# mLSTM cell and leaky-ReLU feed-forward: three gate chunks turned without TensorE, one visit moved ahead of a group's products, a new order of small matmuls, and block sums in single instructions

## The chip, the cores and the metric

The kernel runs on one core of a Trainium2 chip. The metric is device time in microseconds (us) of one execution, lower is better; a time is the median of several executions. Engines are named as in the profile: PE is TensorE's matmul, PEld its weight load, DVE is VectorE, ACT is ScalarE, POOL is GpSimd, and SP is SyncE, which here only issues DMAs. A name with a q (SPq, ACTq) is the queue of an engine, where its DMAs are issued.

## The reference

```python
# q, k, v, o_gate: (4, 8, 768, 40); i_gate, f_gate: (4, 8, 768); fp32
for t in range(S):
    m_new = np.maximum(f_gate[:, :, t] + m, i_gate[:, :, t])
    f_stab = np.exp(f_gate[:, :, t] + m - m_new)
    i_stab = np.exp(i_gate[:, :, t] - m_new)
    m = m_new
    C = f_stab * C + i_stab * outer(v[t], k[t])      # per batch and head, 40 x 40
    n = f_stab * n + i_stab * k[t]
    denom = max(|n . q[t]|, 1)
    y[t] = sigmoid(o_gate[t]) * (C @ q[t]) / denom
# then, with x = y laid out as (3072 tokens, 320):
h = x @ w_in                  # w_in (320, 2048), held in 64-bit floats
out = max(0.01 * h, h) @ w_out  # w_out (2048, 320), held in 64-bit floats
```

## The kernel before

**Stages.** The 768 steps are cut into six chunks c = 0 to 5 of 128 tokens. For each chunk the kernel computes the cell for four batches (a step s = 4c + b is one chunk of one batch, all 8 heads), and one chunk later the feed-forward for the 512 tokens of that chunk (a group g = c - 1). The order of the work of PE, DVE, ACT and POOL is written out by hand: a main loop runs over c, and inside over the positions i of the feed-forward pieces `ffs[i]` of group c - 1. Between pieces it puts visits to the cell work of chunk c. Each engine takes its instructions in this written order. The DMAs of SP are not in that hand-written order once the first chunk is laid out: the framework's scheduler places them.

**Feed-forward.** From group 1 on, both layers are done in a Strassen-Winograd form with seven products. A group has 28 pieces: positions 0 to 13 are the seven first-layer products, each for n = 0 and 1 (`fast_firsts`, matmuls at L986; in groups 2 to 5 the order is p1, p6, p7, p4, p2, p5, p3), and positions 14 to 27 the seven second-layer products (`fast_units`, matmuls at L865). A first-layer product uses the PE array as two tiles of 64 rows by 128 columns: r = 0 and r = 1 are two halves of the output columns, each with its own copy of x and of the weights in its 64 partitions. A second-layer matmul uses the whole array. Every matmul here is fp32 and shows in the trace as two instructions.

x lies in `xT` as five slots of 64 features. The two halves hold the features in different orders (`SLOTS`), so that the pair of blocks K1, K2 and the rest KX of the Strassen form lie in different slots in the two halves. Therefore each sum of blocks takes three instructions (one of 128 partitions for the slot that both halves share, two of 64 for the other). `sums_of_weights` makes 14 DVE instructions once, at the end of chunk 1 (positions 24 on); `sums_of_x(c)` makes 12 POOL instructions (L968) at the last position of each chunk c from 1 on, which p7, p6 and p4 of the next group read (x3, x2, x4; one of the four sums is in place in `xT`). `gather_x` brings x into `xT` by DMA from the scratch `x_dr`, into which the mixes write.

**Cell.** From chunk 2 on a step has two visits. `u_parts(s)` ("parts") does, for the two halves u of 64 tokens, 16 score matmuls (`score`, L661, 40 rows by 64 columns, 64 wide) and 16 matmuls of the carried state (`carried`, L668, 64 rows by 40 columns, 42 wide; only u = 0 in chunk 5) into two PSUM banks `sd`; then DVE multiplies the scores with the decay weights (L680) and adds to the state (L641). `u_mix(s)` ("mix") does 16 matmuls over all rows (L749, tile pT), and DVE, POOL and DMAs bring the result to `x_dr`. A score of half u uses array rows of half 1 - u and array columns of half u; only head 7 goes to the columns of the other half. A carried matmul of half u uses rows and columns of half u. So there are four quadrants of 64 by 64, (row half, column half).

The visits of a chunk are listed by `cell_units` and placed by `pairs`: after position 1 the parts of steps 0 and 1, after 3 their mixes, after 13 the parts of steps 2 and 3, after 17 `u_gates` and the mixes of steps 2 and 3. What a visit needs is made ahead by `ahead(s)`: the exponentials of the decay weights (`prep_exp`, ACT L490), the transposed k and q (`prep_kq`, DVE L545 and L553), the state times its decay (`state_next`, POOL L637) and k times its gate (`prep_vu`, POOL L510).

**Gates.** `gates(c + 1)` (DVE: two scans and a few small operations) and `gates_exp(c + 1)` (four ACT exponentials, then DMAs of the rows to the scratch `a_dr`, from which `w` and `ea` are spread) run with 32 rows, one per batch and head, and the 128 tokens along the free axis. The visits need them with the tokens on the partitions. `gates_T`, called by `u_gates`, transposes them on PE against an identity (tile tg: two kinds at L346, and at L351 the last value of each half, broadcast to all partitions), and two DVE copies bring them to `gT` (L353) and `gL` (L355, a piece of the tile f0). In chunk 0 and for chunk 1 this is done earlier, with three kinds.

**Buffers.** Cell PSUM tiles (sd, tg, pT, tk, tq, hN, xt, xe) share four banks; feed-forward tiles (ph, po) share four others.

Of the kernel before, what the change touches and what calls it, by code (L numbers as in the profile page):

```python
# [19 lines left out]
def kernel(  # L20
# [49 lines left out]
    KC = Dm // DP  # L70
    SLOTS = ([0, 2, 4, 1, 3], [1, 3, 0, 2, 4])
# [214 lines left out]
    x_dr = dr.tile([NS, Dm, P], F32, name="x_dr")  # L286
    gT, gL, dCs = {}, {}, {}
# [31 lines left out]
    def gates_exp(c):  # L319
        sync = nc.sync if c == 1 else queues[0]  # L320
        bu, a, na = bus[c]
        if c == 0:
            nc.scalar.activation(bu[:BH, 1, :], bu[:BH, 0, :], AF.Exp, bias=a[:BH, P - 1 :], scale=1.0)
            return
        for u in range(2):
            at = ts(u, SL)
            last = SL * (u + 1) - 1
            nc.scalar.activation(bu[:, 2, at], a[:, at], AF.Exp, bias=na[:] if u else 0.0, scale=1.0)
            nc.scalar.activation(bu[:, 1, at], bu[:, 0, at], AF.Exp, bias=a[:, last : last + 1], scale=1.0)
        if c > 0:  # L330
            sync.dma_start(a_dr[c, 0].rearrange("u n t -> n u t"), a[:].rearrange("n (u t) -> n u t", u=2))
            if c > 1:
                sync.dma_start(a_dr[c, 1].rearrange("u n t -> n u t"), bu[:, 2, :].rearrange("n (u t) -> n u t", u=2))
            if 1 < c < NB - 2:
                load_fi(c + 2)
# [6 lines left out]
    def gates_T(c, bu):  # L342
        tg = psc.tile([P, 5, BH], F32, name="tg", tag="c")
        kinds = 3 if c == 1 else 2
        for n in range(kinds):
            nc.tensor.transpose(tg[:, n, :], bu[:BH, n, :], ident[:BH, :BH])  # L346
        gT[c] = wk.tile([P, 3, BH], F32, name="gT")
        if c > 0:
            for u in range(2):
                last = SL * (u + 1) - 1  # L350
                nc.tensor.transpose(tg[:, 3 + u, :], bu[:BH, 2, last : last + 1].to_broadcast([BH, P]), ident[:BH, :BH])  # L351
            gL[c] = f0[:, ts(c % 2, 2 * BH)].rearrange("p (u n) -> p u n", u=2)
        nc.vector.tensor_copy(gT[c][:, :kinds], tg[:, :kinds, :])  # L353
        if c > 0:
            nc.vector.tensor_copy(gL[c], tg[:, 3:, :])  # L355

# [286 lines left out]
    def u_parts(s):  # L643
# [14 lines left out]
        def score(h):  # L658
            for u, toks, rows in subs(s):
                to = toks if h < H - 1 else ts(1 - u, SL)  # L660
                nc.tensor.matmul(  # L661
                    bank[1 - u][to, h, :], lhsT=kqT[rows, 0, ts(h, SL)], rhs=kqT[rows, 1, ts(h, SL)], start=True, stop=True,
                )

        def carried(h):
            for u, toks, rows in subs(s):
                if u < ends:
                    nc.tensor.matmul(  # L668
                        dC[u][:, h].rearrange("p k d -> p (k d)"), lhsT=d["ku"][toks, h],
                        rhs=S_v[s % NL][toks, u, h, :, :V1], start=True, stop=True,  # L670
                    )

        behind = iter(range(H))
        for h, n in ((0, 1), (1, 2), (2, 1), (3, 2), (4, 1), (5, 1), (7, 0), (6, 0)):
            score(h)
            for _ in range(n):
                carried(next(behind))
        for u, toks, rows in subs(s):
            for hs, at in ((slice(0, H - 1), toks), (slice(H - 1, H), ts(1 - u, SL))):
                nc.vector.tensor_tensor(mixed(s)[toks, u, hs], w[toks, hs], bank[1 - u][at, hs], op=ALU.mult)  # L680
# [253 lines left out]
    K1, K2, KX = ((0, 3), (0, 2)), ((1, 4), (1, 3)), (2, 4)  # L934
# [4 lines left out]
    alike = [(slice(0, P), 0, 0, 1)] + [(ts(r, DP), 1, K1[r][1], K2[r][1]) for r in range(2)]  # L939

    def sums_of_weights():

        def each(what):
            for rows, k, a, b in alike:
                a11, a12, a21, a22 = (w5[rows, 2 * i : 2 * i + 2, j] for i in range(2) for j in (a, b))
                s2, s3, s4 = (t[rows, :, k] for t in (s2_at, s3_at, s4_at))
                yield {
                    1: lambda: nc.vector.tensor_tensor(a21, a21, a22, op=ALU.add),
                    2: lambda: nc.vector.tensor_tensor(s2, a21, a11, op=ALU.subtract),
                    3: lambda: nc.vector.tensor_tensor(s3, a11, a21, op=ALU.subtract),  # L950
                    4: lambda: nc.vector.tensor_tensor(s4, a12, s2, op=ALU.subtract),
                }[what]()

        for what in (3, 1, 2, 4):
            yield from each(what)
        for r in range(2):
            rows = ts(r, DP)
            yield nc.vector.tensor_tensor(dw[rows], w5[rows, :2, KX[r]], w5[rows, 2:, KX[r]], op=ALU.subtract)

    def sums_of_x(g):  # L960

        xT = st["xT", g]
        for what in range(4):
            for rows, k, a, b in alike:
                b11, b12, b21, b22 = (xT[rows, j, ts(i, HT)] for j in (a, b) for i in range(2))
                x2, x3, x4 = (t[rows, k] for t in (x2_at, x3_at, x4_at))
                to, left, right = ((x3, b22, b12), (b12, b12, b11), (x2, b22, b12), (x4, b21, x2))[what]
                nc.gpsimd.tensor_tensor(to, left, right, op=ALU.subtract)  # L968

    def fast_firsts(g):  # L970
# [21 lines left out]
        def w_at(i, n, at):  # L992
            return [lambda r, k=k: w5[:, 2 * i + n, at[r][k]] for k in range(2)]
# [4 lines left out]
        def x_at(at, h):  # L998
            return [lambda r, k=k: xT[:, at[r][k], ts(h, HT)] for k in range(2)]
# [4 lines left out]
        def rest(i, n, h):  # L1004
            return [(lambda r: w5[:, 2 * i + n, KX[r]] if i < 2 else dw[:, n], lambda r: xT[:, KX[r], ts(h, HT)])]
# [62 lines left out]
    def cell_units(c):  # L1068
# [5 lines left out]
        if c + 1 < NB:  # L1074
            units.insert(2 * B - 2, (u_gates, c + 1))
# [149 lines left out]
    with tc.manual_schedule(engines={E.PE, E.DVE, E.Activation, E.Pool}):  # L1225
# [22 lines left out]
        pairs = (1, 1, 3, 3, 13, 13, 17, 17, 17)  # L1248
# [4 lines left out]
        for c in range(1, NB + 1):  # L1253
# [5 lines left out]
            waiting, after = [], []  # L1259
            for i in range(n_ff):  # L1260
# [14 lines left out]
                for n in masks.get(i, ()) if 1 < c < NB else ():  # L1275
                    if c * B + n < NS:
                        prep_mask(c * B + n)
                ffs[i]()
# [3 lines left out]
                if c == 1 and i >= 24:  # L1282
                    run(sums, 3)
# [7 lines left out]
                if c + 1 < NB:  # L1291
                    if i == (1, 0, 0)[min(c, 3) - 1]:
                        gates(c + 1)
                    if i == (3, 4, 2)[min(c, 3) - 1]:
                        gates_exp(c + 1)
                upto = min(n_c, sum(p <= i for p in (place if c == 1 else pairs)))
                while done < upto:
                    fn, s = cells[done]
                    fn(s)
                    done += 1  # L1300
                    if fn is u_mix:
                        waiting.append(s)
                    if fn is u_plain and s < 2 * B - 1 or fn is u_parts and s == 2 * B - 1:
                        ahead(s + 1)
                    elif fn is u_mix:
                        after.append(s + 2)
                    elif fn is u_plain:
                        prep_mask(s + 2)
                        ahead(s + 2)
# [52 lines left out]
```

## Time and profile before

| | |
|---|---|
| three runs | 482.84, 487.22 and 485.26 us, median 485.26 |
| the profiled execution | 489.31 us, its span 487.5 us |
| mean granted TensorE clock | 0.979 |
| busy share of the span | PE 96%, PEld 86%, DVE 70%, ACT 42%, POOL 37% |
| PE's share of the chain of work that ended last | 88% (L986 32%, L865 32%, L749 3%, L661 2%, L668 1%) |
| start of the first-layer products in the trace | group 1 at 140.2, group 2 at 211.4, group 3 at 281.8, group 4 at 352.5, group 5 at 422.6 us |

All durations below are from the one profiled execution. The idle time of an engine that is not on the chain costs nothing, and PE counts as busy while any of its matmuls is in flight, so a busy PE can still lose time between matmuls; that is read from start times.

### The profile page before, as it was taken

How to read it: one execution, taken by the hardware profiler on the slowest of the kernel's cores; microseconds unless marked ns; L12 is line 12 of the kernel's file. 1: busy time of each engine (PE TensorE's matmuls, PEld its weight loads, DVE VectorE, ACT ScalarE, POOL GpSimd, SP SyncE). 2: the span in 40 equal slices, each digit the busy share in tenths (PEclk: the TensorE clock that was granted, in tenths of full speed). 3: DMA queues.
4: the chain of work that ended last, by engine and by line, in shares of the span. 5: the costliest groups of instructions: out<-in, count | busy, mean ns of one | idle time of the engine just before them, and what ended most of it. 6: DMA issues, size and time to landing. Idle time of an engine off the chain costs nothing.

```text
span 487.5 us, 14191 instructions
## 1 busy us (share of the span) xinstructions
PE 466.8 (96%) x5715; PEld 420.4 (86%) x5715; DVE 339.2 (70%) x597; ACT 203.0 (42%) x488; POOL 181.2 (37%) x241
## 2 busy tenths in 40 slices
PE   8586999979999999999999999999999999999997
PEld 6475898657779899998899988899988899988997
DVE  4667566758989999788788878688757687104631
ACT  3662698844434641246530446420346411153210
POOL 4232524552356422695023784113773003700020
PEclk9897999979999999999999999999999999999999
DMA  9999775988660494576673685674876212200001
GB/s 121 160 180 218 142 211 104 255 151 178 153 159 15 104 199 89 127 165 140 150 151 93 160 172 119 161 144 93 169 146 131 64 50 66 70 1 1 9 8 40
DMA packets 165329, 59.31 MB, mean 122 GB/s; under 512 B 128592, under 2 KB 156048, under 8 KB 165264
## 3 DMA queue, kind: packets, MB, share of 16 engines
q1 hardware_dynamic: 125232, 51.23, 47.5%
q10 hardware_dynamic: 40032, 7.18, 9.1%
q8 instruction: 45, 0.74, 0.7%
q14 instruction: 20, 0.16, 0.1%
HBM read 51.68 MB, written 6.70 MB: 120 GB/s over the span
## 4 chain that ended last, share of the span: by engine, by line
PE 88%; DMA 3%; DVE 3%; SPq 2%; ACT 2%; issue 1%; DVEq 0%; ACTq 0%
PE ph L986 32%; PE po L865 32%; PE ph L808 7%; PE po L830 6%; PE pT L749 3%; PE sd L661 2%; SPq L92 2%; DMA acts<-in_moe_w_in_dram 2%; PE sd L668 1%; PE tk L579 1%; DMA rb<-in_q_dram 1%; DMA qn<-in_q_dram 1%; PE hN L721 1%; DVE w_in L282 1%; PE xe L796 0%
## 5 line engine op out<-in xcount | busy, mean ns | idle before, releaser
L865 PE MATMUL po<-w_out,acts 128*128 128x160 f32 x640 | 89.1, 300 | 0.0
L865 PEld LDWEIGHTS po<-w_out,acts 128*128 128x128 f32 x640 | 87.3, 190 | 0.6 <-ACT acts L1011 0.3
L986 PE MATMUL ph<-xT,w_in 64*128 64x256 f32 x720 | 82.7, 378 | 0.0
L986 PEld LDWEIGHTS ph<-xT,w_in 64*128 64x128 f32 x720 | 69.3, 187 | 8.8 <-issue 1.0
L1015 DVE TENSOR_TENSOR acts<-acts,ph 128x512 f32<-128x512 f32 x60 | 38.4, 683 | 40.4 <-PE ph L986 40.3
L865 PE MATMUL po<-raw,acts 128*128 128x160 f32 x480 | 66.4, 300 | 0.0
L865 PEld LDWEIGHTS po<-raw,acts 128*128 128x128 f32 x480 | 65.4, 190 | 0.3
L637 POOL TENSOR_TENSOR S<-S,f 40x336 f32<-40x336 f32 x36 | 30.9, 859 | 60.0 <-PE hN L721 24.5
L1019 ACT COPY acts<-ph 128x512 f32<-128x512 f32 x60 | 32.1, 586 | 49.0 <-PE ph L986 49.0
L1011 ACT ACTIVATE acts<-acts 128x1024 f32<-128x1024 f32 x30 | 31.7, 1057 | 44.7 <-DVE acts L1015 35.9
L680 DVE TENSOR_TENSOR qn<-w,sd 64x448 f32<-64x448 f32 x80 | 33.5, 418 | 18.0 <-PE sd L661 7.9
L482 POOL TENSOR_TENSOR w<-w,i 128x512 f32<-128x512 f32 x20 | 26.5, 1334 | 51.9 <-DMA w<-a_dr 43.3
L490 ACT ACTIVATE w<-w,gT 128x64 f32<-128x64 f32 x160 | 41.6, 338 | 9.8 <-POOL vu L510 3.6
L808 PE MATMUL ph<-xT,w_in 64*128 64x256 f32 x320 | 38.5, 394 | 1.8 <-DVE w_in L282 1.8
L830 PE MATMUL po<-w_out,acts 128*128 128x320 f32 x128 | 38.9, 457 | 0.0
L808 PEld LDWEIGHTS ph<-xT,w_in 64*128 64x128 f32 x320 | 32.9, 195 | 4.9 <-ACT kqT L596 1.2
L986 PE MATMUL ph<-acts,w 64*128 64x256 f32 x320 | 36.6, 381 | 0.0
L763 POOL TENSOR_TENSOR xb<-xb,den 128x320 f32<-128x320 f32 x16 | 11.6, 728 | 63.6 <-DVE xb L760 63.6
L986 PEld LDWEIGHTS ph<-acts,w 64*128 64x128 f32 x320 | 30.4, 187 | 3.7
L830 PEld LDWEIGHTS po<-w_out,acts 128*128 128x128 f32 x128 | 24.6, 199 | 10.0 <-issue 1.7
L903 POOL TENSOR_TENSOR y<-y,raw 128x160 f32<-128x160 f32 x10 | 9.7, 965 | 56.2 <-DVE acts L905 44.8
L968 POOL TENSOR_TENSOR acts<-xT 64x256 f32<-64x256 f32 (+1 forms) x30 | 24.2, 820 | 11.7 <-ACT xT L797 8.5
(175 smaller groups left out, 757.3 us busy)
## 6 DMA issues: line engine op xcount, KB each, us to landing
rb<-in_k_dram SPq DMA_DIRECT2D x64, 80.0 KB
rb<-in_q_dram SPq DMA_DIRECT2D x64, 80.0 KB
rb<-in_o_gate_dram SPq DMA_DIRECT2D x64, 80.0 KB
ea<-a_dr SPq DMA_DIRECT2D x32, 128.0 KB
raw<-in_moe_w_out_dram SPq DMA_DIRECT2D x6, 640.0 KB
w<-a_dr ACTq DMA_DIRECT2D x24, 128.0 KB
xT<-x_dr SPq DMA_DIRECT2D x32, 96.0 KB
x_dr<-x SPq DMA_DIRECT2D x64, 40.0 KB
```

The lines of the kernel that those rows point to most:

```text
L482: nc.gpsimd.tensor_tensor(w, w, cm2.unsqueeze(1).to_broadcast([P, H, SL]), op=ALU.add)
L490: yield nc.scalar.activation(w[:, h, :], w[:, h, :], AF.Exp, bias=gT[c][:, 0, bh : bh + 1], scale=1.0)
L637: nc.gpsimd.tensor_tensor(new, old, g, op=ALU.mult)
L680: nc.vector.tensor_tensor(mixed(s)[toks, u, hs], w[toks, hs], bank[1 - u][at, hs], op=ALU.mult)
L808: nc.tensor.matmul(ph[r][:, cols], lhsT=w_row(r, slot, j), rhs=xT[DP * r : DP * (r + 1), slot, cols], start=(slot == 0), stop=(slot == KC ...
L830: nc.tensor.matmul(po[n][:], lhsT=acts[:, f, ts(n, P)], rhs=w_out[:, f, :], start=(f == 0), stop=(f == NF - 1),)
L865: nc.tensor.matmul(bank[:], lhsT=left[:, f, :], rhs=right[:, f, :], start=f == 0, stop=f == KH - 1)
L968: nc.gpsimd.tensor_tensor(to, left, right, op=ALU.subtract)
L986: nc.tensor.matmul(bank[r][:, e, :], lhsT=left(r)[rows, e], rhs=right(r)[rows], start=first and e == 0 and m == 0, stop=e == 1 and m == le ...
L1011: nc.scalar.activation(to, z, AF.Prelu, alpha=0.01)
L1015: nc.vector.tensor_tensor(to[:, 2 * r : 2 * r + 2], to[:, 2 * r : 2 * r + 2], bank[r], op=ALU.add)
L1019: nc.scalar.copy(to[:, 2 * r : 2 * r + 2], bank[r])
```

## The change

Four things are changed.

1. **Gates of chunks 3 to 5.** `u_gates` is no longer listed in chunks 2 to 4. In its place `gates_turned(c + 1)`, after position 10, transposes the two kinds with four DVE transposes of 32 x 64 elements, and `gates_exp` sends the last values of each half through DRAM: one DMA writes 64 values to the scratch `g_dr`, a second reads them back to all 128 partitions into the same piece of f0. In chunks 3 and 4 `gates` moves from after position 0 to after position 2 and `gates_exp` from 2 to 3.
2. **First visits.** In chunks 3 to 5 the parts of steps 0 and 1 come before position 0, not after position 1. In chunk 2 they stay.
3. **Order and place of the small matmuls.** The 32 matmuls of a parts visit follow a written list, one for even and one for odd steps, and in the half u = s mod 2 heads 6 and 7 go to the other columns, not head 7 alone. The DVE multiplications at L680 are cut at the same head.
4. **Single Strassen sums.** K1, K2 and KX are the same slots in both halves (0 and 3, 1 and 4, 2), so that the right half now leaves out a different block of features. `sums_of_weights` makes five instructions, one at each position from 24 on, and `sums_of_x` four, each of 128 partitions.

```diff
+    VISITS = (
+        "c01 s01 c00 s00 c11 c10 s11 c21 s10 c20 c31 s21 c30 s20 c41 c40 s31 c51 s30 c50 c61 s41 c60 s40 c71 c70 s51 s60 s50 s71 s61 s70".split(),
+        "s00 c00 s01 c10 c01 s10 c20 c11 s11 s20 c30 c21 s21 c40 c31 s30 c50 c41 s31 s40 c60 c51 s41 c70 c61 s50 s61 c71 s51 s60 s70 s71".split(),
+    )
...
+    g_dr = dr.tile([NB, BH, 2], F32, name="g_dr")
...
             if c > 1:
                 sync.dma_start(a_dr[c, 1].rearrange("u n t -> n u t"), bu[:, 2, :].rearrange("n (u t) -> n u t", u=2))
+                sync.dma_start(g_dr[c], bu[:, 2, :].rearrange("n (u t) -> n u t", u=2)[:, :, SL - 1])
+                to = f0[:, ts(c % 2, 2 * BH)]
+                sync.dma_start(to, g_dr[c].rearrange("n u -> (n u)").partition_broadcast(P))
+                gL[c] = to.rearrange("p (n u) -> p u n", u=2)
...
+    def gates_turned(c):
+
+        bu = bus.pop(c)[0]
+        g = gT[c] = wk.tile([P, 3, BH], F32, name="gT")
+        for j in range(P // BH):
+            nc.vector.transpose(g[ts(j, BH), :2, :], bu[:, :2, ts(j, BH)])
...
+        to = [[toks if h < 7 - (u == s % 2) else ts(1 - u, SL) for h in range(H)] for u, toks, _ in subs(s)]
...
-        behind = iter(range(H))
-        for h, n in ((0, 1), (1, 2), (2, 1), (3, 2), (4, 1), (5, 1), (7, 0), (6, 0)):
-            score(h)
-            for _ in range(n):
-                carried(next(behind))
+        parts = list(subs(s))
+        for what, h, u in VISITS[s % 2]:
+            {"s": score, "c": carried}[what](int(h), *parts[int(u)])
...
-    K1, K2, KX = ((0, 3), (0, 2)), ((1, 4), (1, 3)), (2, 4)
+    K1, K2, KX = slice(0, 4, 3), slice(1, 5, 3), 2
...
+        a11, a12, a21, a22 = (w5[:, 2 * i : 2 * i + 2, at] for i in range(2) for at in (K1, K2))
+        yield nc.vector.tensor_tensor(s3_at, a11, a21, op=ALU.subtract)
+        yield nc.vector.tensor_tensor(a21, a21, a22, op=ALU.add)
+        yield nc.vector.tensor_tensor(s2_at, a21, a11, op=ALU.subtract)
+        yield nc.vector.tensor_tensor(s4_at, a12, s2_at, op=ALU.subtract)
+        yield nc.vector.tensor_tensor(dw, w5[:, :2, KX], w5[:, 2:, KX], op=ALU.subtract)
...
+        b11, b12, b21, b22 = (xT[:, at, ts(i, HT)] for at in (K1, K2) for i in range(2))
+        for to, left, right in ((x3_at, b22, b12), (b12, b12, b11), (x2_at, b22, b12), (x4_at, b21, x2_at)):
+            nc.gpsimd.tensor_tensor(to, left, right, op=ALU.subtract)
...
-        if c + 1 < NB:
-            units.insert(2 * B - 2, (u_gates, c + 1))
         return units
...
-        pairs = (1, 1, 3, 3, 13, 13, 17, 17, 17)
+        first_pairs = (1, 1, 3, 3, 13, 13, 17, 17)
+        pairs = (-1, -1, 3, 3, 13, 13, 17, 17)
...
+                if i == 0:
+                    visits(-1)
                 ffs[i]()
...
                 if c == 1 and i >= 24:
-                    run(sums, 3)
+                    run(sums, 1)
...
-                    if i == (1, 0, 0)[min(c, 3) - 1]:
+                    if i == (1, 0, 2)[min(c, 3) - 1]:
                         gates(c + 1)
-                    if i == (3, 4, 2)[min(c, 3) - 1]:
+                    if i == (3, 4, 3)[min(c, 3) - 1]:
                         gates_exp(c + 1)
...
+                if c > 1 and i == 10:
+                    gates_turned(c + 1)
+                visits(i)
```

`visits(i)` is the old code that ran the visits due at position i, made a function; `first_pairs` is used in chunk 2 and `pairs` in chunks 3 to 5.

## The prediction

> **What bounds the kernel now.** I read the table of stretches first, with borders at the starts of the groups (columns: us, then busy time and instructions of PE, PEld, DVE, ACT, POOL, then clock, DMA share, GB/s).
>
> ```profile
> 105.00:140.00 35.00, 35.00 (x255) 24.55 (x254) 28.29 (x46) 17.49 (x49) 10.51 (x14) 0.95 0.76 154
> 140.00:211.35 71.35, 71.00 (x901) 66.15 (x900) 63.46 (x105) 27.84 (x71) 35.83 (x43) 1.00 0.54 122
> 211.35:281.84 70.49, 70.49 (x901) 65.78 (x900) 56.66 (x101) 27.53 (x70) 31.54 (x38) 1.00 0.64 140
> 281.84:352.52 70.68, 70.68 (x901) 65.97 (x900) 57.16 (x100) 27.43 (x70) 30.57 (x37) 1.00 0.65 141
> 352.52:422.61 70.09, 70.09 (x833) 65.42 (x832) 44.98 (x80) 22.55 (x50) 26.69 (x36) 1.00 0.40 92
> ```
>
> From 105 to 422.6 us PE is idle for 0.35 us in all, at full clock from 140 (what it is idle behind that is the end of the kernel, which the change doesn't touch). So a DVE or POOL instruction saved buys nothing unless PE waits for it, and each us taken out of PE's own stream is a us of the time. The chain of waits (start, us, what) says the same of the middle of chunk 3:
>
> ```profile
> 248.72 8.89 PE po L865 x64
> 257.61 0.24 PE tg L346 x2
> 257.85 0.12 PE tg L351 x2
> 257.97 2.02 PE pT L749 x64
> 259.98 21.93 PE po L865 x160
> ```
>
> Inside PE's stream three things are left to gain: the tg transposes, the joints between kinds of matmul, and the packing of sd. I take these from start times of single matmuls, since their ends are modelled.
>
> **Part 1, gates off PE.** The timeline of PE in chunk 2:
>
> ```profile
> 186.49 0.30 PE L346 MATMUL tg<-ident,bu 32*128 32x32 f32 x2
> 186.64 0.28 PE L351 MATMUL tg<-ident,bu 32*128 32x32 f32 x2
> 186.84 1.15 PE L749 MATMUL pT<-qn,S 128*64 128x64 f32 x32
> 188.34 1.15 PE L749 MATMUL pT<-qn,S 128*64 128x64 f32 x32 [0.35 <-DVE f L355]
> 189.43 0.81 PE L865 MATMUL po<-raw,acts 128*128 128x160 f32 x4
> ```
>
> From the first tg to the first pT pass 0.351, 0.358 and 0.351 us in chunks 2, 3 and 4. The joint po to tg (0.230 us between starts) is as long as po to pT in chunk 5 (0.229), so these 1.06 us go whole. In chunk 2 alone the second mix waits for tg's PSUM bank, which DVE empties late: its 64 pT take 2.43 us from first to last start against 1.86 elsewhere. Without tg there is no such bank: 0.57 us more. Sum 1.63 us. What could be late next is L919 of DVE, which p7 needs: in chunk 2 its first half ends about 197.1 and p7 would come at 198.2 - 0.9 = 197.3; it just fits, and a miss costs 0.2 us.
>
> The cover of what is added: four DVE transposes of 32x64 per chunk. The nearest rows are a 128x64 copy (L353, 222 ns) and a 128x512 transpose (L545, 693 ns, so about 90 for an eighth): 0.4 to 0.9 us, less the two copies gone (0.43). At position 10 DVE idles 0.58 us before its next add (312.42 in chunk 4) and 1.2 to 1.3 before the ones behind; the bank that this add reads is written again 1 us after its end. I take nothing; if that cover failed, 0.3 us a chunk. The gates' own DVE work (282.2 to 286.1, 3.9 us) moves behind the multiplications of the first two parts, which come earlier: these end at about group start + 5.6 us, the gates at + 9.5, and the mixes want DVE at + 10.4. It fits.
>
> The two new DMAs stand on SP's queue behind the two of a_dr and ahead of load_fi and the eight x_dr writes; the read waits there until the write has landed. SP issues each DMA in 0.3 to 0.6 us, so 0.8 to 1.0 us, plus the wait. No row has such a write; the nearest is x_dr: its last write issued at 339.5, the read that needs it went at 344.6. So the wait is 0 (if the scheduler puts other DMAs between) to 4.7 us. Behind it stand the x_dr writes, then rb, ea and the gathers. SP itself stops at 319.3 to 323.2 in chunk 4, and the gather that matters ends at 347.4, for a group that starts at 352.5. I take nothing, and the rest is a rival. The Trainium skill, "DMA: Bandwidth & Descriptors", on the anatomy of a DMA, gives a fixed cost of about 2.0 us, mostly the receipt of the write (its fit is for GpSimd's path); by it the wait would be 2 us, and that rival would weigh less than half.
>
> **Part 2, first visits moved.** A joint costs by the kinds on its sides: po to ph 229 ns between starts, ph to sd 306, sd to ph 148; two ph steps in one mode are 209 apart, and the first pair of ph after another kind is followed after 320 instead of 216 ns. Before: po, p1, sd, p6. After: po, sd, p1, p6. The joint ph to sd (306) becomes a plain step (209), and one of two slow first pairs (104) goes; po to sd is not in the trace, and I take po to pT's 229. Gain 97 + 104 = 0.20 us, in chunks 3, 4 and 5: 0.60 us. Bounds: 0.3 if po to sd costs 306, 0.8 if it costs sd's 148.
>
> The cover: at 281.8 all that the parts read is there. Exponentials ended at 280.2, the last kqT at 279.6, the last vu (POOL L510) at 276.3; in chunk 5 350.3, 350.3 and 347.0 for a start at 352.5. These follow PE's own second-layer products, so they move with it. The move also delays p6, which reads x2 of the single sums. In chunk 5 these are at their limit today (POOL's timeline, third line is x2):
>
> ```profile
> 350.49 3.06 POOL L968 TENSOR_TENSOR acts<-xT 128x256 f32<-128x256 f32 x3 [1.60 <-DMA rb<-in_o_gate_dram]
> 353.63 2.20 POOL L968 TENSOR_TENSOR xT<-xT 128x256 f32<-128x256 f32 x3
> 355.91 2.21 POOL L968 TENSOR_TENSOR acts<-xT 128x256 f32<-128x256 f32 x3
> ```
>
> They end at 358.1, p6 starts at 357.95 and gets its second slot just in time.
>
> **Part 4, single sums.** POOL: 12 of about 0.8 us become 4 of 128x512. Nearest rows: L482, 128x512, 1.27 us here; two of today's, 1.6. So 9.6 us become 5.1 to 6.4. DVE's 14 (130.2 to 140.6) become 5, about 4 x 1.3 (128x1024, L886 to L919) + 0.9 = 6 us. PE waits for neither today: worth 0. But x2 would be ready 2.3 to 3.5 us before p6.
>
> **Part 3, order of sd.** In one quadrant scores start every 58 ns and carried every 37 ns (per instruction). Before, the two score quadrants carry 14 x 58 = 812 ns a visit, the other two 16 x 37 + 2 x 58 = 708; a pair of visits is at least 1624. Measured from first to last start, the pairs take 1760, 1666, 1668, 1631, 1734 and 1761 ns in chunks 2 to 4 and 1630 twice in chunk 5, which has 96 instructions, not 128. So the score quadrants bind, and not the number of instructions; the excess is the order. After, even and odd visits swap loads: score quadrants (12 + 14) x 58 = 1508 a pair, the others 32 x 37 + 6 x 58 = 1532. With 20 to 60 ns of imperfection I take 1570 against a mean of 1703 (0.13 us by 6) and 1550 against 1630 (0.08 by 2): 0.96, call it 1.0 us. Bounds: -0.3 (a list whose head-of-line blocking is worse than today's) and 1.3. The four single visits of chunk 1 gain nothing: 12 or 14 scores and at most 824 in the other quadrants. The Trainium skill, "TensorEngine Tiling (Array Packing)", on instruction overhead, speaks against this part: about 60 cycles each, so that a narrow matmul lasts like one of 60 columns. By that a carried one costs as much as a score, the new bound would be 38 x 58 = 2204 ns a pair, and today's 36 x 58 = 2088. The measured 1630 to 1761 and the 37 ns refute it here.
>
> **Sum.** 1.63 + 0.60 + 1.0 = 3.2 us. The profiled execution took 489.31 (span 487.5), 4.05 above the median of 485.26; by it the after is 486.1. I put the same saving on the median: **482.1 us**, 0.7% less.
>
> **Rivals.** (a) The new order brings nothing, PE's issue having its own rhythm: 2.2 us saved, 483.0. For: pairs with one list scatter by 130 ns; against: the pairs at 1630 sit exactly on the score bound. Chance 0.15.
> (b) Slower: the read of g_dr blocks SP for 4.7 us, and the delay reaches the gather of x in each of chunks 2 to 4. The sums would end 4.7 us later, with 2.3 to 3.5 us of room before p6: up to 2.4 us of stall three times, 7.2 - 3.2 = +4.0, 489.3. It decides once more than 2.3 us of delay reach the gather. For: SP issues almost without pause, and the gather of chunk 4 went at 347.4. Against: its pause of 3.9 us at 319.3. Chance 0.07, of which a part over +1% needs ACT's queue, where the loads of w wait for a_dr, to slip as well.
> (c) The scheduler places SP's DMAs anew. In chunk 1 PE waits 3.0 us for q at 102.2, whose issue took 2.66 us, and the clock drops behind it. Gone, it is 482.1 - 3 = 479.1; as much longer, 485.1. For: part 3 and the five sums alter the instructions around; against: none of the DMAs there is changed. Chances 0.11 and 0.05.
> (d) The sums or gates do not get off PE's path as said (a bank or DVE late in each of three chunks, 0.5 us each): 482.1 + 1.5 = 483.6. For: L919's thin room in chunk 2; against: no such wait in chunks 3 and 4 today. It shares (a)'s chance.
>
> The forecast, 482.1 within about 1.3, has 0.62. The range reaches down to (c) and up to between (c) and (b): 479.4 to 485.6. About 1% (4.9 us, what three runs spread over 4.4 can tell) bounds the verdict: faster, under 480.4, 0.18 ((c) and the good end of the bounds); slower, over 490.1, 0.06 ((b) with ACT); same 0.76.
>
> **What would show it.** No tg on PE in chunks 2 to 4, and po followed at once by 64 pT within 1.9 us, in chunk 2 too. From the last po of one group to that of the next 69.6 to 69.9 us in groups 2, 3 and 4, which start 70.1 to 70.7 apart now. Pairs of sd at 1.53 to 1.6 us from first to last start, right behind the last po. x2 done 2 us or more before p6. SP may stand 2 to 5 us before the read of g_dr, with no PE wait after it. Wrong would be: PE idle at a group's start (p1 or p6 for DMA or POOL), sd pairs at 1.7 us, or a moved wait at 102 us that outweighs the rest.

## The result and the profile after

| | before | after |
|---|---|---|
| median | 485.19 us (6 runs, 482.84 to 488.41) | 510.05 us (6 runs, 505.79 to 513.06) |
| ratio | | 1.0506, 95% interval 1.0464 to 1.0548 |
| the profiled execution's span | 487.5 us | 511.2 us |
| mean granted TensorE clock | 0.979 | 0.950 |

The kernel became 25 us slower; 3 us less had been forecast. The two profiles are of executions that took 4.1 us (before) and 3.0 us (after) more than these medians. The same table of stretches as in the prediction (columns: us, busy time and instructions of PE, PEld, DVE, ACT, POOL, then clock, DMA share, GB/s), with the borders at the starts of the groups of the kernel after, says where:

```profile
149.20:229.20 80.00, 74.00 (x897) 69.13 (x896) 60.26 (x99) 27.67 (x71) 31.84 (x33) 0.94 0.50 111
229.20:299.20 70.00, 70.00 (x900) 65.60 (x899) 56.79 (x104) 26.19 (x65) 27.75 (x29) 1.00 0.64 133
299.20:376.40 77.20, 73.23 (x897) 68.64 (x896) 57.69 (x102) 28.57 (x76) 26.83 (x31) 0.96 0.65 134
376.40:446.40 70.00, 70.00 (x836) 65.52 (x834) 44.92 (x80) 22.55 (x50) 23.00 (x24) 1.00 0.41 96
```

Chunks 3 and 5 have no idle PE and are shorter than before, as forecast. In chunk 2 PE is idle for 6.0 us and in chunk 4 for 3.97. Right after each idle time the granted clock is lower (0.50 from 193 to 196 us in chunk 2; 0.94 and 0.96 over the two stretches), so that the loss is larger than the idle time: in chunk 2 the next 64 po take 11.45 us, where 64 po took 8.89 in the prediction's chain of waits. Measured from the start of the last po of a group to that of the next (the first column is the start of the last po ahead of group 1):

| us | up to group 1 | chunk 2 | chunk 3 | chunk 4 | chunk 5 | the last group |
|---|---|---|---|---|---|---|
| before | 139.8 | 71.32 | 70.49 | 70.68 | 70.09 | 61.91 |
| after | 148.8 | 80.20 | 69.94 | 77.32 | 69.83 | 61.91 |

What PE waited for is in its table of waits (us in total, times, longest):

```profile
PE tk L595 <- DMA rb<-in_q_dram: 8.8, 2, 5.1
PE xt L812 <- DVE x L725: 8.8, 3, 5.8
PE sd L677 <- issue: 6.0, 1, 6.0
PE po L881 <- DVE acts L935: 3.8, 1, 3.8
```

tk waits in chunk 1 for loads of q (3.0 us in the kernel before), sd in chunk 2, po in chunk 4; xt is in chunk 0 and was there before (8.0). The 6.0 us of sd stand at "issue": between two matmuls of one visit PE waits for no semaphore that the profile shows.

```profile
186.67 6.00 issue
192.68 0.29 PE sd L677
```

What ends just before is a transfer of 16 KB on the queue that the page calls "instruction" (q8): it runs from 189.30 to 191.29 us, and PE goes on 1.4 us later. It is the 17th transfer on that queue. In all six kernels with the write of this change (below) PE stops at the same count of its matmuls (the 2240th in the trace, in one of them the 2241st) and goes on 1.4 to 1.5 us after the transfer has ended. In the others it had ended 1.5 us or more before PE came there, and PE stands at most 0.16 us. So I read the 6.0 us as PE waiting for its own instructions, which are late with the other DMAs; no run tests that alone.

The table of waits of SP's queue has a row that is new:

```profile
SPq L96 <- DMA g_dr<-bu: 30.4, 4, 8.8
```

Four times SP stands before the read of g_dr for the write to land, 7.6 us on average. It is four times and not three: `gates_exp(2)`, in chunk 1, issues the pair too, though the copy from PE's transposes overwrites that gL. The chain of waits in chunk 4 (start, us, what) follows the delay to PE:

```profile
316.55 3.61 DMA S<-in_v_dram
320.17 9.69 DMA g_dr<-bu
...
329.92 4.39 DMA f<-g_dr
...
335.71 4.58 DMA rb<-in_o_gate_dram
...
343.57 6.46 DMA ea<-a_dr
...
359.00 1.22 DVE acts L935
360.22 0.14 issue
360.36 1.67 PE po L881 x5
```

The write of 256 bytes lands 9.69 us after its issue, and everything behind it on the queue comes late; in the end DVE is late with the sum that a second-layer product reads. The packets of 4 bytes themselves take 0.007 to 0.009 us each.

Part 1's step on PE went as planned. In the chain of waits of chunk 3, tg is gone between po and pT:

```profile
266.42 8.89 PE po L881 x64
275.31 2.02 PE pT L765 x64
277.32 4.68 PE po L881 x33
```

### The profile page after: what moved, and what is told of

It reads as the page before. It is cut to its first block, busy times and chain, and to the rows that moved or that the text cites. A ratio compares the mean times of both kernels' runs of the same rounds, so it can differ in the third digit from the quotient of the medians.

```text
span 511.2 us, 14138 instructions
## 1 busy us (share of the span) xinstructions
PE 475.0 (93%) x5703; PEld 428.6 (84%) x5703; DVE 333.5 (65%) x594; ACT 202.6 (40%) x488; POOL 159.9 (31%) x201
## 4 chain that ended last, share of the span: by engine, by line
PE 77%; DMA 12%; SPq 3%; DVE 3%; issue 2%; POOL 1%; ACT 1%; DVEq 0%; POOLq 0%; ACTq 0%
PE po L881 28%; PE ph L988 27%; PE po L846 6%; PE ph L824 6%; DMA rb<-in_q_dram 4%; SPq L96 3%; PE pT L765 3%; PE sd L677 3%; DMA g_dr<-bu 2%; DMA acts<-in_moe_w_in_dram 1%; DMA ea<-a_dr 1%; DMA S<-in_v_dram 1%; PE tk L595 1%; DMA rb<-in_o_gate_dram 1%; DMA f<-g_dr 1%
## 5 line engine op out<-in xcount | busy, mean ns | idle before, releaser
L881 PE MATMUL po<-w_out,acts 128*128 128x160 f32 x640 | 91.6, 305 | 0.0
L881 PEld LDWEIGHTS po<-w_out,acts 128*128 128x128 f32 x640 | 89.9, 194 | 0.7 <-ACT acts L1013 0.3
L988 PE MATMUL ph<-xT,w_in 64*128 64x256 f32 x720 | 82.7, 378 | 0.0
L988 PEld LDWEIGHTS ph<-xT,w_in 64*128 64x128 f32 x720 | 69.2, 187 | 8.6 <-issue 0.6
L881 PE MATMUL po<-raw,acts 128*128 128x160 f32 x480 | 69.6, 308 | 3.8 <-DVE acts L935 3.8
L881 PEld LDWEIGHTS po<-raw,acts 128*128 128x128 f32 x480 | 68.3, 197 | 4.3 <-ACT y L918 4.0
L506 ACT ACTIVATE w<-w,gT 128x64 f32<-128x64 f32 x160 | 41.5, 339 | 38.7 <-DMA rb<-in_k_dram 12.6
L498 POOL TENSOR_TENSOR w<-w,i 128x512 f32<-128x512 f32 x20 | 27.6, 1390 | 78.6 <-DMA w<-a_dr 56.6
L694 DVE TENSOR_TENSOR qn<-w,sd 64x384 f32<-64x384 f32 (+1 forms) x80 | 33.5, 418 | 27.2 <-ACT w L506 10.8
L824 PE MATMUL ph<-xT,w_in 64*128 64x256 f32 x320 | 41.2, 414 | 1.6 <-DVE w_in L286 1.6
L824 PEld LDWEIGHTS ph<-xT,w_in 64*128 64x128 f32 x320 | 34.6, 207 | 6.1 <-ACT kqT L612 1.2
L846 PEld LDWEIGHTS po<-w_out,acts 128*128 128x128 f32 x128 | 24.6, 199 | 10.0 <-issue 1.3
L569 DVE TENSOR_TENSOR qn<-kqT,ea 64x512 f32<-64x512 f32 x32 | 27.6, 862 | 0.8
```

The source lines that it names most:

```text
L498: nc.gpsimd.tensor_tensor(w, w, cm2.unsqueeze(1).to_broadcast([P, H, SL]), op=ALU.add)
L506: yield nc.scalar.activation(w[:, h, :], w[:, h, :], AF.Exp, bias=gT[c][:, 0, bh : bh + 1], scale=1.0)
L569: nc.vector.tensor_tensor(mixed(s)[rows, 1 - r], d["kqT"][rows, 1].rearrange("p (h t) -> p h t", t=SL), d["ea"][rows], op=ALU.mult,)
L824: nc.tensor.matmul(ph[r][:, cols], lhsT=w_row(r, slot, j), rhs=xT[DP * r : DP * (r + 1), slot, cols], start=(slot == 0), stop=(slot == KC ...
L846: nc.tensor.matmul(po[n][:], lhsT=acts[:, f, ts(n, P)], rhs=w_out[:, f, :], start=(f == 0), stop=(f == NF - 1),)
L881: nc.tensor.matmul(bank[:], lhsT=left[:, f, :], rhs=right[:, f, :], start=f == 0, stop=f == KH - 1)
```

## The experiments

### Is it the gates at all

**Gates back on PE**: the kernel after, with `gates_T` as before and without the four transposes, so parts 2 to 4 alone.

```diff
-                sync.dma_start(g_dr[c], ...)
-                sync.dma_start(to, g_dr[c]...partition_broadcast(P))
+            units.insert(2 * B - 2, (u_gates, c + 1))
```

> The changed kernel with its gates turned on PE again: no scratch g_dr, u_gates at position 17; the moved first visits, the new order and the single sums stay. Theory 1 (the way of the last gate values through DRAM costs the time: its write completes 9.7 to 10 us after its issue and the read behind it holds SP for 8 to 9 us, four times): all of the 25 us go, 483 to 486 us, before less the 0.6 us of the moved visits. Theory 2 (the moved visits, the order or the sums make PE wait): it stays above 500 us.

Measured: 484.15 us, ratio 0.9983 (0.9952 to 1.0015). **Part 1 alone** on the kernel before, with `gates` and `gates_exp` at their old positions:

> The kernel before with the gates' part of the change alone: four DVE transposes and the two DMAs through g_dr; first visits, order and sums as before. Theory 1: 503 to 511 us, with PE stalls in chunks 1, 2 and 4 as in the changed kernel. Theory 2: 483.6 us, the 1.6 us of tg saved.

Measured: 502.26 us, ratio 1.0366 (1.0338 to 1.0394), chunks 2 to 5 at 79.91, 70.18, 70.26 and 70.68 us; chunk 4 loses nothing here, against the expectation. So the loss is in part 1. The rest of part 1 was cleared by **no g_dr**: the kernel after, with gL of chunks 3 to 5 from the tile `ea`, which holds the same numbers, by a POOL copy of 128x8 per step.

```diff
-                sync.dma_start(g_dr[c], ...)
-                sync.dma_start(to, g_dr[c]...partition_broadcast(P))
+            if s >= 3 * B:
+                gl = st[s]["gl"] = wk.tile([P, H], F32, name="gl", bufs=4)
+                nc.gpsimd.tensor_copy(gl[:], st[s]["ea"][:, :, SL - 1])
```

> The changed kernel with both g_dr DMAs taken out. The last gate values of chunks 3 to 5 are copied by POOL (128x8, one copy a step) from the tile ea, which already holds them on the right partitions; for chunk 2 they come from PE, as in both kernels. The four DVE transposes stay. Theory 1: 482 to 484 us (before less 1.6 for tg and 0.6 for the joints, at most 0.3 for the order). Theory 3 (the transposes on DVE, or the gates being later, cost): above 490 us.

Measured: 482.30 us, ratio 0.9965 (0.9941 to 0.9990): everything but the two DMAs is harmless, and this kernel has the lowest median of all. The table of stretches, from group 1 on, has no idle PE and no lowered clock:

```profile
134.60:205.40 70.80, 70.80 (x898) 65.91 (x896) 58.82 (x98) 27.74 (x71) 32.06 (x35) 1.00 0.53 124
205.40:275.40 70.00, 70.00 (x898) 65.67 (x896) 57.37 (x105) 27.85 (x71) 28.19 (x34) 1.00 0.64 142
275.40:345.30 69.90, 69.90 (x898) 65.56 (x896) 55.83 (x103) 27.53 (x70) 26.57 (x34) 1.00 0.66 141
345.30:415.20 69.90, 69.90 (x834) 65.55 (x833) 45.39 (x81) 22.55 (x50) 22.51 (x26) 1.00 0.40 94
```

**The same round trip as one row**: a DVE transpose of two 32x32 blocks puts the 64 values into one partition, and the write is one piece of 256 bytes; write, wait and read stay where they are.

```diff
-                sync.dma_start(g_dr[c], bu[:, 2, :]...[:, :, SL - 1])
+                nc.vector.transpose(row, bu[:, 2, :]...)
+                sync.dma_start(g_dr[c].rearrange("u n -> (u n)").unsqueeze(0), row[BH - 1 : BH]...)
```

> The changed kernel with the same two DMAs at the same places in SP's queue, but what is written is one row: two DVE transposes of 32x32 put the 64 last values on one partition, and the write is 256 bytes in one piece instead of 64 pieces of 4 bytes. Theory 1a (it is the 64 small writes that complete late): the write completes in about 1.5 to 2 us as those of a_dr and x_dr do, SP is held for 1 to 2 us, 482 to 487 us. Theory 1b (any write and read through DRAM in SP's queue holds it as long): SP still held 8 us, 500 us or more.

Measured: 483.68 us, ratio 0.9987 (0.9960 to 1.0013). The read goes 1.24 to 1.72 us after the write's issue (8.0 to 10.2 in the kernel after). A round trip through DRAM on SP's queue is therefore not the trouble; this write is.

### Is it SP's wait, or the write itself

So far all fits a queue held by its wait. Two kernels take the wait for the data away and leave the write: **read late**, with the read moved to product 10, behind load_fi and the x_dr writes (three reads, since that for chunk 2 falls away), and **write only**, without any read (gL as in "no g_dr").

```diff
-                sync.dma_start(to, g_dr[c]...partition_broadcast(P))
+        queues[0].dma_start(to, g_dr[c]...partition_broadcast(P))
```

> The changed kernel with the read of g_dr moved from its place right behind the write to the turning of the gates (product 10 of the group), so that SP issues load_fi and the x_dr writes in between; none for chunk 2, whose gL comes from PE. The writes of 64 pieces of 4 bytes stay, four of them. The output stays the same. If SP's standing before the read is the harm (theory 1): 482 to 486 us, the writes still completing 8 to 10 us after their issue, and the stretches of chunks 2 and 4 at 70 to 71 us instead of 80 and 77. If the slow write also holds up the DMAs behind it (rival): 495 us or more, with PE still waiting for rb in chunk 1.

> The changed kernel with the four writes of g_dr kept, without the reads; gL of chunks 3 to 5 from the ea tile by a 128x8 copy of POOL per step, as in the run 'ea'. Theory 1 (only the wait of the read costs): the time of 'ea', 482.3 us, within 1%. Rival (the 64 small pieces themselves hold up other DMAs): over 488 us, and rb of chunk 1 lands late as in the changed kernel.

Measured: 500.52 us, ratio 1.0335 (1.0299 to 1.0372) for read late, and 500.62 us, ratio 1.0339 (1.0304 to 1.0374) for write only. Theory 1 fell: without the read most of the loss stays. The table of stretches of write only, in pieces of 2 us, shows what the write does (issued at 169.12 us, the last completion at 179.1; the two last columns are DMA share and GB/s):

```profile
168.10:170.10 2.00, 2.00 (x22) 1.78 (x22) 1.96 (x3) 0.24 (x1) 0.10 (x1) 1.00 0.62 156
...
172.10:174.10 2.00, 2.00 (x22) 2.00 (x20) 1.86 (x7) 1.40 (x3) 0.00 (x0) 1.00 0.20 6
174.10:176.10 2.00, 2.00 (x20) 1.71 (x18) 2.00 (x3) 0.00 (x0) 0.00 (x0) 1.00 0.08 15
176.10:178.10 2.00, 2.00 (x24) 1.51 (x24) 2.00 (x4) 0.00 (x0) 0.00 (x0) 1.00 0.06 7
178.10:180.10 2.00, 1.28 (x88) 1.14 (x88) 2.00 (x3) 0.11 (x1) 0.00 (x0) 1.00 0.01 4
180.10:182.10 2.00, 0.00 (x0) 0.00 (x0) 1.89 (x6) 1.90 (x5) 0.00 (x0) 1.00 0.31 89
```

From 172 to 180 us all 16 DMA engines together move 4 to 15 GB/s, though SP had issued six more loads by 172.4 us and ACT one (w<-a_dr, 170.43). By the semaphore updates in the trace SP's first two land 9.0 and 9.5 us after their issue, its other four and ACT's 12.2 to 13.4. Even the other queue stands. Then SP itself stops, with nobody reading g_dr:

```profile
SPq L96 <- DMA g_dr<-bu: 17.8, 3, 6.3
```

Its next DMA is issued at 179.12 us, when the write has completed; it takes over the write's semaphore, so I read the row as a wait for that semaphore to come free (from the numbers in the trace; no kernel tested it).

**Write apart** is write only, with 512 bytes between the 64 values.

```diff
-    g_dr = dr.tile([NB, BH, 2], F32, name="g_dr")
+    g_dr = dr.tile([NB, BH, 2, P], F32, name="g_dr")
...
+                sync.dma_start(g_dr[c, :, :, 0], ...)
```

> As 'write_only', but each of the 64 values of 4 bytes goes to a place of its own, 512 bytes from the next; before, they stood in 512 bytes together. If the pieces are slow since they fall into the same few lines of memory, all 16 completions come within 2 to 3.5 us of the issue, as those of the a_dr writes; if each piece of 4 bytes is slow by itself, the last still comes at 8 to 10 us. Time 482 to 484 us under either.

Measured: 483.43 us, ratio 0.9971 (0.9941 to 1.0002): 17.2 us less than write only, by nothing but the addresses. (Before, the 64 values stood in 256 bytes, not in 512 as the expectation has it.) The same table of stretches, with the write issued at 164.78 us:

```profile
163.80:165.80 2.00, 2.00 (x22) 1.80 (x20) 1.94 (x4) 0.31 (x1) 0.05 (x1) 1.00 0.58 151
...
167.80:169.80 2.00, 2.00 (x22) 1.82 (x20) 1.89 (x6) 1.25 (x3) 0.00 (x0) 1.00 0.87 212
169.80:171.80 2.00, 2.00 (x20) 1.81 (x18) 2.00 (x3) 1.60 (x5) 0.00 (x0) 1.00 0.68 176
171.80:173.80 2.00, 2.00 (x27) 1.64 (x28) 2.00 (x4) 0.76 (x2) 0.00 (x0) 1.00 0.65 173
```

173 to 212 GB/s at the same distance from the write, and no idle PE. So the 64 small pieces, lying next to each other, all but stop the DMA engines by themselves.

### How far apart must they be

The distance was then taken down to 64, 32 and 8 bytes, with the same edit (shown for 64), and in **pairs** DVE first brings the 32x2 values together, so that 32 pieces of 8 bytes fill the 256 bytes.

```diff
-    g_dr = dr.tile([NB, BH, 2, P], F32, name="g_dr")
+    g_dr = dr.tile([NB, BH, 2, 16], F32, name="g_dr")
...
+                nc.vector.tensor_copy(g2[:], bu[:, 2, :]...[:, :, SL - 1])
+                sync.dma_start(g_dr[c], g2[:])
```

> As 'write_apart' (483.4 us, all completions 1.6 to 2.7 us after the issue), but the 64 values of 4 bytes stand 64 bytes from one another instead of 512. What is asked is the size of the stretch of memory that two pieces must not share. If it is 64 bytes or less: as 'write_apart', 16 completions within 3 us, time 481 to 486 us. If it is 128 to 512 bytes: completions up to 4 to 10 us after the issue and a time of 488 to 500 us.

> As 'write_64' (483.4 us, all completions within 1.9 us of the issue), with 32 bytes between the 64 values. If the stretch that pieces must not share is 64 bytes long, two pieces share one now and the last completion comes later, at 2 to 4 us, with little effect on the time (483 to 487 us). If it is 32 bytes or less, it is as 'write_64'.

> As 'write_64', with 8 bytes between the 64 values of 4 bytes; in 'write_only' (4 bytes apart, 500.6 us) the last completion comes 9.5 to 10 us after the issue. If the wait grows with the number of pieces that share a stretch: half as many share one, last completion at 4 to 6 us, time 485 to 495 us. If it is a fixed cost of pieces whose stretch is shared at all: 9 to 10 us and about 500 us.

> As 'write_only', but DVE first copies the 32x2 values into a tile of their own, so that the write has 32 pieces of 8 bytes, with no gap between them in DRAM. If each piece costs about 0.15 us in turn (10 us for 64): last completion at about 5 us, time 487 to 495 us. If the length of the stretch in DRAM decides (256 bytes as before): 9 to 10 us and about 500 us.

The last completion after the issue, from the trace's semaphore updates, for the four writes in turn (a write in pieces has 16 completions, of which the trace holds 15 for the fourth of write only; the one row has two):

| write | us | time, ratio |
|---|---|---|
| 64 of 4 bytes, 4 apart (write only) | 9.5, 10.0, 9.5, 8.4 | 500.62, 1.0339 (1.0304 to 1.0374) |
| 64 of 4 bytes, 8 apart | 3.1, 4.3, 4.6, 3.3 | 485.36, 1.0022 (0.9985 to 1.0059) |
| 32 of 8 bytes, 8 apart (pairs) | 4.5, 3.9, 4.5, 3.7 | 486.07, 1.0021 (0.9983 to 1.0059) |
| 64 of 4 bytes, 32 apart | 1.8, 1.8, 1.8, 2.0 | 483.26, 0.9982 (0.9951 to 1.0014) |
| 64 of 4 bytes, 64 apart | 1.8, 1.8, 1.8, 1.9 | 483.43, 0.9980 (0.9942 to 1.0018) |
| 64 of 4 bytes, 512 apart | 2.7, 1.8, 2.0, 2.2 | 483.43, 0.9971 (0.9941 to 1.0002) |
| one of 256 bytes (one row) | 1.1, 1.2, 1.5, 1.6 | 483.68, 0.9987 (0.9960 to 1.0013) |

From 32 bytes on, nothing is left of it; that pieces 32 bytes apart still disturb each other, as in a shared stretch of 64 bytes, is ruled out. Neither the number of pieces alone (64 at 32 bytes: 1.8 us) nor the length in DRAM alone (256 bytes as 64 pieces: 8.4 to 10.0, in pairs: 3.7 to 4.5) makes the time. What fits all rows is the number of pieces that share a stretch of at most 32 bytes: if it is 32 bytes long, eight pieces in it cost 8 to 10 us, four 3 to 4.6, one 1.8 to 2.7. It isn't proportional. No distance between 8 and 32 bytes was run, and what happens inside the memory or the engines no run shows. The Trainium skill, "DMA: Bandwidth & Descriptors", in its specifications, says that below 512 bytes the engine reads, modifies and writes. All these pieces are below that, and the completions of the 4-byte ones differ by a factor of five, so that rule alone doesn't give the loss; that several such updates of one stretch go one after another would fit both.

### Why 510 and not 500

With the read gone the loss is 17 us, in the kernel after 27 (against write apart). **Gates early** is the kernel after with `gates` and `gates_exp` in chunks 3 and 4 (not in chunk 3 alone, as the expectation has it) at their old positions:

```diff
-                    if i == (1, 0, 2)[min(c, 3) - 1]:
+                    if i == (1, 0, 0)[min(c, 3) - 1]:
...
-                    if i == (3, 4, 3)[min(c, 3) - 1]:
+                    if i == (3, 4, 2)[min(c, 3) - 1]:
```

> The changed kernel with one difference: in chunk 3 the gates and their exponentials stand at products 0 and 2 of the group again, where the kernel before has them, and not at 2 and 3. The output stays the same. Question: why the slow write costs nothing in the last group before chunk 4 in the run 'only_gates' (70.26 us) and 7 us in the changed kernel (77.32). If the place of the write decides (theory 2: at 320 us the standstill of the DMAs meets the loads of the next chunk that have no room left, at 310 us it doesn't): the stretch of chunk 4 falls to 70 to 71 us and the time to 502 to 505 us. If it is the first visits themselves, which want their data earlier (rival): it stays at 76 to 78 us and the time at 508 to 511 us.

Measured: 499.58 us, ratio 1.0319 (1.0273 to 1.0365), chunk 4 at 70.50 us. So what the same write costs is not fixed: chunk 4 takes 70.50 us with the gates at the old positions, 77.32 with them two and one positions later, and 69.94 at the later positions with the read moved (read late). But the later position with the read right behind the write isn't enough for the loss: the next run, "not for chunk 2", has both, and its chunk 4 takes 69.95. Counted from the last po ahead of chunk 4, its write goes at 21.2 us in the kernel after and at 20.6 to 20.8 in gates early, part 1 alone and the next run; from the write's issue to the read it is 9.8 us in the first and 6.9 to 9.1 in the others. What decides between them no run shows. The other 3.7 us between the medians are not from chunk 4. The profiles differ most ahead of chunk 3, where this edit changes nothing: the last po ahead of group 1 starts at 148.8 us in the kernel after, at 142.2 here, 145.0 in part 1 alone and 141.5 in write only, and chunk 2 takes 80.20, 78.54, 79.91 and 79.60. In the twelve profiles without this write it starts at 132.8 to 139.8 us. What spreads chunk 1 stays open.

**Not for chunk 2** drops the pair that has no use.

```diff
-                sync.dma_start(g_dr[c], ...)
+                if c > 2:
+                    sync.dma_start(g_dr[c], ...)
```

> The changed kernel with the pair of DMAs of g_dr issued for chunks 3 to 5 only; the one for chunk 2, in chunk 1, has no use, since gL[2] is overwritten by the copy from PE's transposes. Theory 1: the 7 us lost in chunk 1 come back, those of chunks 2 and 4 stay: 502 to 504 us, chunk 1's stretch at 112 to 114 us instead of 120.9. Rival (chunk 1 lost by something else, the single sums or the new order of sd): 508 us or more.

Measured: 497.83 us, ratio 1.0302 (1.0226 to 1.0377). More than the 7 us came back: the last po ahead of group 1 starts at 134.7 us (14 earlier), chunk 4 is at 69.95, but chunk 3, free before, is at 74.22 and chunk 2 at 81.46. Three standstills instead of four, each falling elsewhere: the stalls can't be added up from the kernel with four.

### Parts 2, 3 and 4

Parts 2 and 3, each alone on the kernel before, with their edits as in the change:

> The kernel before with part 2 alone, the first two visits of a group in front of its first product, in chunks 3 to 5, and the gates of chunk 4 at products 2 and 3. As predicted 0.2 us a chunk: 484.2 us, and the stretches of chunks 3, 4 and 5 each 0.2 us shorter than 70.49, 70.68 and 70.09. Rival: the visits' data come later than PE wants them, and the time is 484.8 us or more.

> The kernel before with part 3 alone, the new order of the scores and carried products. As predicted (1.0 us): 483.5 us, pairs of sd at 1.57 us in chunks 2 to 4. Rival (a), the order brings nothing: 484.8 us within 0.5, pairs at 1.66 to 1.75 us as before.

Part 2 alone: 484.08 us, ratio 0.9988 (0.9966 to 1.0009), chunks 3 to 5 at 70.38, 70.46 and 69.89 us, 0.11, 0.22 and 0.20 less. Part 3 alone: 484.74 us, ratio 1.0004 (0.9981 to 1.0028). Part 4 was not run alone. The last run takes part 3 out of the best kernel, "no g_dr":

> The run 'ea' (gates off PE without g_dr; 482.3 us) with the old order of the scores and carried products. As the run 'only_order' says (the order is worth 0.1 us): 482.3 us within 0.6. As predicted for part 3: 483.3 us. Pairs of sd at 1.63 us and more, instead of 1.61 in 'ea'.

Measured: 483.50 us, ratio 0.9985 (0.9954 to 1.0015), beside 0.9965 (0.9941 to 0.9990) with the new order. The median lies near the number for "as predicted", but the intervals overlap, the two were run beside different runs of the kernel before, and chunks 2 to 5 together differ by 0.45 us in the two traces (281.06 and 280.61). The pairs of visits, from first to last start in ns, say more (chunks 2 to 5, two pairs each):

| list | pairs | mean |
|---|---|---|
| old (before) | 1760 1666 1668 1631 1734 1761 1630 1630 | 1685 |
| old (best kernel, old order) | 1760 1668 1806 1631 1824 1762 1630 1630 | 1714 |
| new (part 3 alone) | 1811 1611 1609 1610 2113 1745 1603 1603 | 1713 |
| new (best kernel) | 1812 1609 1758 1611 1707 1609 1602 1602 | 1664 |

An undisturbed pair takes 1609 ns with the new list and 1630 with the old. The first pair of chunks 2 to 4 takes 1.67 to 1.82 us with the old list and, but for one of 1.61 and one of 2.11, 1.71 to 1.81 with the new.

## Why the prediction was wrong

**The step that failed** is "I take nothing, and the rest is a rival", on the wait for the write of g_dr, with its bounds of 0 to 4.7 us from the x_dr row. Measured: 8.0 to 10.2 us from the write's issue to the read, four times. And the wait was only part of it: without any read (write only) 17 of the 27 us stay, because the write holds up the other DMAs, for which the sum had no term. The row chosen as nearest was a row of writes of another kind: those of x_dr and a_dr have long pieces (a_dr's 256 bytes each), and the last completion of a_dr's comes 1.5 to 3.6 us after the issue in chunks 1 to 4 of the kernel after. 64 pieces of 4 bytes side by side have no near row in the trace of before, and the bound should have said so. The cover was wrong too: a pause of 3.9 us in SP's row covers a late SP, not 16 DMA engines that move next to nothing for 8 us. The fourth write, which stands in the diff, was not seen at all: `c > 1` takes in the call for chunk 2.

**The 2 us for a write.** The Trainium skill, "DMA: Bandwidth & Descriptors", on the anatomy of a DMA, gives a fixed cost of about 2.0 us (fitted on GpSimd's path). The runs here come near it for the one row of 256 bytes (1.1 to 1.6 us) and for pieces 32 bytes apart (1.8 to 2.0), and are at four to five times of it for the write as it was (7.9 to 10.2 in the kernel after). The prediction named it as a reason to give rival (b) less weight, for the one write that it doesn't hold for.

**Rival (b)** had the place, the round trip of g_dr, but not the mechanism or the size. It had one queue blocked and the gather of x late in three chunks, at +4.0 us; what came was a standstill of both queues, which reached PE by the loads of q in chunk 1, as read above by PE's own instructions in chunk 2, and by a DVE sum in chunk 4. (ACT waits 12.6 us for DMAs in chunk 2 as well, but till 193.35 us, when PE has been going again since 192.68.) It cost 25 us and the gain of the other parts, so that the range, which took in a share of (b), ended 24 us too low.

**Part 1's gain** was right to the last digit. From the last po before pT to the first matmul behind it, the kernel before takes 3163, 2603 and 2596 ns in chunks 2 to 4, and 2244 or 2245 in the kernel after and the best one: 0.92 + 0.36 + 0.35 = 1.63 us. In "no g_dr", with the four DVE transposes, PE has no wait from group 1 to the end of group 4. Chunk 2's whole stretch there shrank by 0.50 us only, though: the 208 ph between its visits take 23.09 us, 22.65 in the kernel before. In profiles that keep the gates on PE they take 22.65 (gates back on PE) to 23.40 (part 3 alone), so this is scatter between profiles. The four transposes take 0.98 us a chunk (0.4 to 0.9 were taken).

**Part 2**: po to sd is 229 ns, as taken, ph to sd is gone at the moved visits, and the stretches of part 2 alone shrink by 0.11 to 0.22 us: 0.53 us for 0.60.

**Part 3** was mis-sized, and rival (a) was right on the size. Forecast were 0.96 us for the eight pairs; together they take 13.48 and 13.71 us with the old list, 13.71 and 13.31 with the new. The bound of 1508 or 1532 ns let the light quadrants of one visit fill up with the next one's work. They do not, as far as the starts tell: in an undisturbed pair of the new list the first visit's carried products have all started by 624 ns, from there to 797 only scores start, and half of the instructions have started after 813 ns. That is near the 14 x 58 = 812 of the fullest quadrant of a single visit, and 2 x 812 = 1624 is near both 1609 and 1630. Rival (a)'s reason, a rhythm of PE's issue, does not fit: in chunk 5 a pair has 96 instructions instead of 128 and takes 1602 ns all the same. Swapping the quadrants between visits is worth 21 ns a pair.

**Part 4** gained room and no time. POOL's timeline of "no g_dr" at the place of the lines shown of before (the third line is x2):

```profile
344.31 1.27 POOL L968 TENSOR_TENSOR acts<-xT 128x512 f32<-128x512 f32 x1 [2.20 <-DVE qn L564]
345.66 1.60 POOL L968 TENSOR_TENSOR xT<-xT 128x512 f32<-128x512 f32 x1
347.34 1.27 POOL L968 TENSOR_TENSOR acts<-xT 128x512 f32<-128x512 f32 x1
```

and PE's, where p6 is the second line:

```profile
349.73 1.25 PE L986 MATMUL ph<-xT,w_in 64*128 64x256 f32 x10
350.81 2.54 PE L986 MATMUL ph<-acts,w 64*128 64x256 f32 x22
```

x2 is done at 348.61 us, 2.2 us before p6 (2.3 to 3.5 forecast). The four sums take 5.4 us here (5.1 to 6.4 forecast), and DVE's five sums of weights 6.0, as forecast.

**The sum without the fault.** The four parts without the round trip ("no g_dr") give 482.30 us, or 0.35% less than before (0.1% to 0.6%). That this is near the 482.1 of the forecast is in part luck, since part 3 brought less than its 1.0 us: against the kernel before as run beside it (484.55) it is 2.2 us less, which is what rival (a) has for parts 1 and 2. By the profiles chunks 2 to 5 became 2.0 us shorter (282.58 to 280.61). So the terms of parts 1 and 2, worked out from rows of the trace, held, that of part 3 was too large, and the forecast was lost by one that had no row.

## What to carry to other kernels

Before a DMA is costed at its latency, look at its pieces in DRAM: neighbouring pieces of 4 bytes, written here from 32 partitions, all but stop both queues for 8 us, where the same values 32 bytes apart, or as one row made by a transpose, land in under 2 us. Where an engine stands with no semaphore to wait for, look for the transfers of its instructions in the list of DMA queues. Count what a new instruction's condition takes in, call by call. And a bound from the "nearest row" is worth only as much as the row is like it: where size of piece or pattern differ by 64 times, keep the upper end open and run the piece alone.

## What the runs showed of the hardware

- The 64 writes of 4 bytes in 256 bytes complete 7.9 to 10.2 us after the issue (kernel after and write only), 8 bytes apart 3.1 to 4.6, 32 apart 1.8 to 2.0, while their packets take 0.007 to 0.009 us each. DMAs of both queues, issued 1.3 to 3.3 us behind one in write only, land 12.2 to 13.4 us after their issue.
- Where the 17th transfer on the queue of instructions ends late, PE stops at one and the same matmul for 3.3 to 6.3 us and goes on 1.4 to 1.5 us after its end (six kernels with the write).
- SP waits for such a write also where nothing reads what it wrote (6.3 us at most, write only).
- After PE had been idle for 6 us in chunk 2 the granted clock was 0.50 from 193 to 196 us, and 64 po took 11.45 us instead of 8.89.
- Two visits of small matmuls in four quadrants take 1609 ns as a pair, near twice the 812 of the fullest quadrant of one, where the loads summed over both would allow 1532.
